# Attention and a two-layer feed-forward block on one core: GpSimd's steps of a head moved to 5 and 7, and the first weights' conversion spread over a pair's 18 steps

## The chip, the core and the metric

The kernel runs on one core of a Trainium2 chip. The metric is the device time of one execution in microseconds (us). The engines are PE (matrix products), DVE, ACT, POOL (GpSimd) and SP (which here only issues DMAs). Each engine works through its own queue in order and waits on semaphores for the others.

## The reference, cut to what matters

All tensors are float64 at the interface; the kernel reads them as pairs of 32-bit words and computes float32-like products from pieces.

```python
# q, k, v: (4, 8, 1152, 64): 32 heads of 1152 keys, 576 pooled queries, 64 channels
q_pool = q.reshape(B, H, S // 2, 2, D).mean(axis=3)
scores = scale * q_pool @ k.T          # 576 x 1152 per head
scores = scores - scores.max(-1)       # softmax over the keys
attn = exp(scores); attn = attn / (attn.sum(-1) + 1e-09)
x = (attn @ v)                         # laid out as 2304 tokens x 512
h = x @ w_in                           # 512 -> 2048
g = s * relu(h) ** 2 + b
out = g @ w_out                        # 2048 -> 512
```

## The kernel before

Heads are worked in 16 pairs. A head is nine steps of 128 keys (`j` = 0 to 8), a pair 18 steps, the attention 288 steps (`n`) and three more to drain. Below, "step 12" means `n % 18 == 12`. The order of every instruction is written out by hand: the main loop over `n` emits them, and `later(k, fn)` with `tick()` puts a piece of work a few steps behind.

In a step PE makes the scores of 128 keys against 576 queries (`score_step`, L486, tile `s`, two buffers of two PSUM banks), one or two products for the row maxima of the pair after this one (`max_unit`, L456, tile `m`, reduced by DVE at L457 into `pm`), and the value products of the step three before (`value_step`, tile `o`, `LAG` = 3). `KIND` says how a step's exponentials are split into a high and a low part:

- "v": ACT makes `ph` (L495) and the full exponential in place in `s` (L498), DVE subtracts to `pl` (L501). Six value products: L524, L526, L528 for each half of the queries.
- "g": ACT makes `ph` and the full exponential `pe` in SBUF, POOL subtracts to `pl`. The same six products.
- "w" (a whole step): ACT makes only `pe` (L490), and PE multiplies it unsplit (L518).

L528 is the product that reads `pl`. At a head's last value product `finish` (steps 2 and 11) has ACT copy the outputs out of PSUM in four pieces (`xu`, `l`, L544 and L545). DVE and POOL then make the inverse and the scaled output (`lt`, `rc`, `rr`, and POOL's `xo` at L564, once per pair).

The pair two ahead is prepared at the steps in `PREP`: DVE transposes (`ka`, `kb`, `qt`), POOL copies and subtracts (`qs` L412, `kh`, `kl` L419, `qh`, `qz`, `ql` L420). `ql` subtracts in place in `qT`. `qm` is a small ACT copy out of `qT` (L212) that the maxima of that pair's first rows need. POOL also splits the values of the next head at steps 7 and 16 (`vv`, `vl`, `prep_v`). SP issues the loads: `kraw` and `qraw` at step 14, `vf` at steps 3 and 12.

In the last six pairs (10 to 15) the loop also converts the first three blocks of float64 weights, one chunk of 128 x 512 numbers per pair. `weights_a()` fetches a chunk one pair ahead (L134, tile `wst`) and runs `narrow` on the one at hand. Its pieces `s0` to `s5` come at the steps in `STA`, counted from the call (0 and 1 both fall in the call's own step, k in the step k - 1 behind). `CB` and `CP` set the calls: step 4 of each of these pairs. So `s0` (ACT: `whm`, `wR`) is at step 4, `s1`, `s1b`, `s1c` (DVE: L159, L163, L166) at step 7, `s2` (DVE L169, ACT L170) at step 9, and POOL's three pieces `s3` (L174), `s4` (L177), `s5` (L180) at steps 12, 14 and 16. Each scratch tile has one buffer.

After the attention the feed-forward block follows (`Moe`), with its own conversion (`weights_b`, `STB`).

Of the kernel before, what the change touches and what calls it, by code (L numbers as in the profile page):

```python
# [12 lines left out]
AF = mybir.ActivationFunctionType  # L13
# [18 lines left out]
KB = 384  # L32


KIND = "vwvgvwvgw" * 2

PP = (("ka", 0), ("kb", 0), ("ha", 0), ("hb", 1), ("qs", 1), ("qt", 1), ("qm", 2), ("qh", 2), ("qz", 2), ("kl", 2), ("ql", 3), ("l0", 7))
PREP = (("qs", 9), ("ka", 10), ("kb", 11), ("ha", 11), ("qt", 12), ("hb", 12), ("kl", 12), ("qm", 13), ("qh", 13), ("qz", 13), ("ql", 14), ("l0", 4), ("l1", 13))
LR = 14
LD = 1  # L40
VS = (7, 16)
XT = (1, 2, 3, 4, 8)
SW = (3, 9)
CB, CP = 274, 18
WB = (7, 11)
STA = (0, 4, 4, 4, 6, 9, 11, 13)
STB = (0, 1, 2, 3, 4, 5, 6, 8)
MO = (2, 3, 6)
XS = (1, 2)
# [3 lines left out]
def f32(ap):  # L53
    return ap.bitcast(F32)
# [3 lines left out]
def attention_moe_kernel(ctx: ExitStack, tc: tile.TileContext, q, k, v, w_in, w_out, s_in, b_in, out):  # L58
    nc = tc.nc
# [35 lines left out]
    def weight_tiles(pool, f0, f1):  # L95
        n = f1 - f0
        ih = pool.tile([P, NC, n * P], F32R, name=f"wih{f0}")
        il = pool.tile([P, NC, n * P], F32R, name=f"wil{f0}")
        oh = pool.tile([P, n, DM], F32R, name=f"woh{f0}")
        ol = pool.tile([P, n, DM], F32R, name=f"wol{f0}")  # L100
        for i in range(n):
            f = f0 + i
            wi_hi[f] = ih[:, :, i * P:(i + 1) * P]
            wi_lo[f] = il[:, :, i * P:(i + 1) * P]
            wo_hi[f] = oh[:, i, :]
            wo_lo[f] = ol[:, i, :]

    def conversions(pool, stage, f0, f1, bufs, stages, psum=None):

        weight_tiles(pool, f0, f1)
        chunks = []
        for f in range(f0, f1):
            chunks.append((w_in[:, f * P:(f + 1) * P].rearrange("(c p) f -> p c f", p=P), wi_hi[f], wi_lo[f], f"i{f}"))
            chunks.append((w_out[f * P:(f + 1) * P, :].rearrange("p (c f) -> p c f", c=NC),
                           wo_hi[f].rearrange("p (c f) -> p c f", c=NC), wo_lo[f].rearrange("p (c f) -> p c f", c=NC), f"o{f}"))
        wide = w_in.dtype == mybir.dt.int64
        raw = {}  # L120
        state = [-1]

        def done(i):
            f = f0 + i // 2
            ready[f] = ready.get(f, 0) + 1

        def tmp(tag, name):
            return stage.tile([P, NC, P], F32, tag=tag, bufs=bufs, name=f"{tag}{name}")

        def fetch(i):  # L130
            src, _, _, name = chunks[i]
            if wide:
                raw[i] = stage.tile([P, NC, 2 * P], I32, tag="wst", bufs=2, name=f"wst{name}")
                nc.sync.dma_start(raw[i], src.bitcast(I32))  # L134
            else:
                raw[i] = stage.tile([P, NC, P], F32, tag="wst", bufs=2, name=f"wst{name}")
                nc.sync.dma_start(raw[i], src)

        def narrow(i):
            _, hi, lo, name = chunks[i]  # L140
            words = raw.pop(i).rearrange("p c (n w) -> p c n w", w=2)
            high, low = words[:, :, :, 1].bitcast(F32), words[:, :, :, 0].bitcast(U32)
            hm, ab, A, R = (tmp(t, name) for t in ("whm", "wab", "wA", "wR")) if psum is None else (None, *(tmp(t, name) for t in ("wab", "wA", "wR")))

            bank = None if psum is None else psum.tile([P, 512], F32, tag="w", bufs=1, name=f"w{name}").rearrange("p (c f) -> p c f", c=NC)
            hm, bits, full = (hm, ab, A) if psum is None else (bank, bank, bank)
            hmi, biti, abi, fulli, top = (t.bitcast(I32) for t in (hm, bits, ab, full, high))
            eng = nc.gpsimd if psum is None else nc.vector

            def s0():  # L150
                nc.scalar.activation(hm, high, AF.Abs)
                if psum is None:
                    nc.scalar.activation(R, low, AF.Copy, scale=2.0 ** -52)
                else:
                    nc.gpsimd.tensor_scalar(out=R, in0=low, scalar1=2.0 ** -52, scalar2=0.0, op0=ALU.mult, op1=ALU.add)

            def s1():

                nc.vector.tensor_scalar(out=hm, in0=hm, scalar1=W_MIN, scalar2=W_MAX, op0=ALU.max, op1=ALU.min)  # L159

            def s1b():

                nc.vector.tensor_scalar(out=biti, in0=hmi, scalar1=0x07FFFFFF, scalar2=3, op0=ALU.bitwise_and, op1=ALU.logical_shift_left)  # L163

            def s1c():
                nc.vector.scalar_tensor_tensor(out=fulli, in0=top, scalar=-0x40000000, in1=biti, op0=ALU.bitwise_and, op1=ALU.bitwise_or)  # L166

            def s2():
                nc.vector.tensor_scalar(out=abi, in0=fulli, scalar1=-0x800000, scalar2=None, op0=ALU.bitwise_and)  # L169
                nc.scalar.activation(hi, full, AF.Copy)  # L170

            def s3():

                nc.gpsimd.tensor_tensor(out=R, in0=R, in1=ab, op=ALU.mult)  # L174

            def s4():
                eng.tensor_tensor(out=A, in0=full, in1=f32(hi), op=ALU.subtract)  # L177

            def s5():
                nc.gpsimd.tensor_tensor(out=lo, in0=A, in1=R, op=ALU.add)  # L180
                done(i)

            for at, fn in zip(stages, (s0, s1, s1b, s1c, s2, s3, s4, s5)):
                later(at, fn)

        def split(i):
            _, hi, lo, _ = chunks[i]
            st = raw.pop(i)
            nc.scalar.activation(hi, st, AF.Copy)

            def rest():
                nc.gpsimd.tensor_tensor(out=lo, in0=st, in1=f32(hi), op=ALU.subtract)
                done(i)

            later(stages[4], rest)

        def go():
            i = state[0]
            if i >= len(chunks):
                return False  # L200
            if i + 1 < len(chunks):
                fetch(i + 1)
            if i >= 0:
                (narrow if wide else split)(i)
            state[0] += 1
            return True

        return go
# [12 lines left out]
    def later(k, fn):  # L221
        step[1] += 1
        queue.append((step[0] + k, step[1], fn))
# [106 lines left out]
    qm = ap.tile([P, P], F32R, name="qm")  # L330
# [149 lines left out]
    def score_step(hd, j, kind):  # L480
        assert holds["k", hd % 3] == holds["c", hd % 3] == hd
        kk, qq = kks[hd % 3], qqs[hd % 3]
        ps = ps_s.tile([P, 2, 512], F32, tag="s", name=f"s{hd}_{j}")
        for a in range(2):
            for i in range(2):
                nc.tensor.matmul(ps[:, a, :HALF], kk[:, i, j * P:(j + 1) * P], qq[:, i, a], start=(i == 0), stop=(i == 1))  # L486
        if kind != "v":
            pe = late.tile([P, 2, HALF], F32, tag="pe", bufs=PE, name=f"pe{hd}_{j}")
        if kind == "w":
            nc.scalar.activation(pe, ps[:, :, :HALF], AF.Exp, scale=SCALE)  # L490
            prob[hd, j] = pe, None
            return
        ph = late.tile([P, 2, HALF], F32R, tag="ph", bufs=PB, name=f"ph{hd}_{j}")
        pl = late.tile([P, 2, HALF], F32R, tag="pl", bufs=PB, name=f"pl{hd}_{j}")
        nc.scalar.activation(ph, ps[:, :, :HALF], AF.Exp, scale=SCALE)  # L495

        full = ps[:, :, :HALF] if kind == "v" else pe
        nc.scalar.activation(full, ps[:, :, :HALF], AF.Exp, scale=SCALE)  # L498
        prob[hd, j] = ph, pl
        eng = nc.vector if kind == "v" else nc.gpsimd  # L500
        fresh.append(lambda: eng.tensor_tensor(out=pl, in0=full, in1=f32(ph), op=ALU.subtract))  # L501
# [115 lines left out]
    lays = {}  # L617
    weights_a = conversions(wa, wstage, 0, SW[0], 1, STA)
    NS = NH * NJ

    for n in range(NS + LAG):
# [5 lines left out]
        for part in ORD[at] if at is not None else "sff":  # L627
            if part == "s" and n < NS:
                score_step(hd, j, KIND[n % 18])
            elif part == "f":  # L630
# [10 lines left out]
        if n < NS:  # L641
# [4 lines left out]
            if n == LD:  # L646
                load_k(2)
                load_q(2)
            if n % 18 == PREP[0][1]:
                lays = {k: prep[k] for k in ("l0", "l1") if k in prep}  # L650
                prep = prep_pair(p + 2) if p + 2 < NPAIR else {}
            for name, at in PREP:

                ops = prep if name not in ("l0", "l1") or at < PREP[0][1] else lays
                if n % 18 == at and name in ops and n >= 8:
# [96 lines left out]
```

## Time and profile before

| | us |
|---|---|
| three runs, median (lowest to highest) | 973.78 (971.0 to 974.75) |
| the profiled execution's own time | 976.95 |
| its span, first to last instruction | 975.2 |
| PE busy in the span | 922.3 (95%) |
| DVE, ACT, POOL busy | 627.0, 545.9, 507.5 |
| PE busy in 20 to 350 us (330 us, pairs without conversion) | 317.55 |
| PE busy in 350 to 525 us (175 us, with conversion) | 158.68 |

The attention runs from about 20 to 557 us, the feed-forward block from there to the end. Where PE is busy nearly all of the time, an idle engine elsewhere costs nothing; what counts is each place where PE stands still, and what it stands still for. A row such as "PE o L528 <- POOL pl L501" says that PE's product at line 528 waited for POOL's subtraction at line 501.

### The profile page before, as it was taken

To read this page: it belongs to the slowest core of one execution; us is meant where nothing else is said; L and a number is where in the kernel's file an instruction comes from. 1 tells how busy PE (TensorE), PEld (TensorE's weight loads), DVE (VectorE), ACT (ScalarE), POOL (GpSimd) and SP (SyncE) were. 2 spreads that over 40 slices of the span, in tenths; PEclk is the share of its full clock that TensorE was granted. 3 is DMA by queue.
4 is the path that set the end of the run, shared out by engine and by line. 5 is a ranking of instruction groups with operands and counts; after the bars stand their busy time and mean duration, and the time that the engine had idled before them with its cause. 6 is when DMAs were issued, how large, how long until landed. Compare 5 with 4: busy or idle time off the path is not lost.

```text
span 975.2 us, 16173 instructions
## 1 busy us (share of the span) xinstructions
PE 922.3 (95%) x5712; PEld 821.4 (84%) x5712; DVE 627.0 (64%) x1168; ACT 545.9 (56%) x1054; POOL 507.5 (52%) x405
## 2 busy tenths in 40 slices
PE   4999999999999998988989989999999999999998
PEld 3888888888888887877877877889999899999997
DVE  5777776777677776876875376776776653334333
ACT  2766666666676675665767755554444443333332
POOL 6567656665667568568665567665353430110000
PEclk9999999999999999999999999999999999999999
DMA  8878776777767776676754155663544332222211
GB/s 149 167 145 169 158 152 122 154 168 147 134 138 167 156 152 147 153 142 138 165 146 102 35 162 164 205 217 130 174 130 158 104 136 78 66 87 90 84 44 44
DMA packets 255312, 131.17 MB, mean 135 GB/s; under 512 B 203776, under 2 KB 227328, under 8 KB 255232
## 3 DMA queue, kind: packets, MB, share of 16 engines
q1 hardware_dynamic: 244512, 129.62, 55.0%
q10 hardware_dynamic: 10720, 0.52, 0.7%
q8 instruction: 46, 0.75, 0.3%
q14 instruction: 34, 0.28, 0.1%
HBM read 68.68 MB, written 18.87 MB: 90 GB/s over the span
## 4 chain that ended last, share of the span: by engine, by line
PE 67%; ACT 12%; POOL 7%; DVE 5%; DMA 3%; issue 3%; ACTq 1%; SPq 0%; DVEq 0%; POOLq 0%
PE h L272 18%; PE y L299 17%; PE s L486 12%; PE o L518 5%; PE m L456 5%; PE o L524 4%; PE o L528 4%; PE o L526 4%; ACT ph L495 3%; ACT xu L544 2%; ACT l L545 2%; ACT s L498 2%; POOL pl L501 1%; DVE pm L457 1%; DMA wsto<-in_moe_w_out_dram 1%
## 5 line engine op out<-in xcount | busy, mean ns | idle before, releaser
L457 DVE TENSOR_REDUCE pm<-m 128x1 f32<-128x384 f32 x432 | 230.6, 549 | 112.8 <-PE m L456 106.9
L486 PE MATMUL s<-qq,kk 128*128 128x288 f32 x1152 | 217.6, 311 | 10.9 <-ACT pe L498 7.8
L272 PE MATMUL h<-x,wih 128*128 128x256 f32 x1152 | 213.3, 283 | 7.1 <-DVE gl L286 6.0
L272 PEld LDWEIGHTS h<-x,wih 128*128 128x128 f32 x1152 | 186.0, 189 | 22.1 <-DVE gl L286 6.4
L495 ACT ACTIVATE ph<-s 128x576 fp32r<-128x576 f32 x192 | 125.2, 652 | 132.4 <-PE s L486 109.8
L486 PEld LDWEIGHTS s<-qq,kk 128*128 128x128 f32 x1152 | 175.6, 191 | 27.2 <-ACT pe L498 11.0
L501 POOL TENSOR_TENSOR pl<-pe,ph 128x576 fp32r<-128x576 f32 x64 | 91.5, 1429 | 141.8 <-ACT pe L498 131.2
L272 PE MATMUL h<-x,wil 128*128 128x256 f32 x576 | 162.2, 282 | 0.0
L456 PE MATMUL m<-kh,qz 128*128 128x384 f32 x384 | 156.9, 418 | 3.2 <-DVE pm L457 3.1
L253 POOL TENSOR_TENSOR x<-xr,x 128x1024 fp32r<-128x1024 f32 x27 | 65.0, 2406 | 152.0 <-ACT x L212 143.1
L280 DVE SCALAR_TENSOR_TENSOR h<-h,sb,r 128x256 f32<-128x256 f32 x144 | 70.2, 487 | 114.5 <-ACT r L289 114.5
L524 PE MATMUL o<-ph,vv 128*128 128x288 f32 x384 | 119.0, 310 | 7.8 <-issue 4.8
L518 PE MATMUL o<-pe,vf 128*128 128x288 f32 x384 | 126.0, 412 | 0.0
L528 PE MATMUL o<-pl,vv 128*128 128x288 f32 x384 | 113.6, 296 | 7.3 <-POOL pl L501 7.3
L289 ACT ACTIVATE r<-h 128x256 f32<-128x256 f32 x144 | 55.6, 386 | 110.0 <-PE h L272 109.8
L501 DVE TENSOR_TENSOR pl<-s,ph 128x576 fp32r<-128x576 f32 x128 | 96.2, 752 | 30.9 <-ACT s L498 24.7
L526 PE MATMUL o<-ph,vl 128*64 128x288 f32 x384 | 113.6, 296 | 0.0
L299 PE MATMUL y<-wol,gh 128*128 128x512 f32 x288 | 113.1, 393 | 0.0
L299 PE MATMUL y<-woh,gl 128*128 128x512 f32 x288 | 112.9, 392 | 0.0
L299 PE MATMUL y<-woh,gh 128*128 128x512 f32 x288 | 112.6, 391 | 0.0
L272 PEld LDWEIGHTS h<-x,wil 128*128 128x128 f32 x576 | 109.6, 190 | 0.0
L283 ACT ACTIVATE gh<-h,sb 128x256 fp32r<-128x256 f32 x144 | 68.0, 473 | 64.6 <-DVE h L280 64.3
(89 smaller groups left out, 1508.6 us busy)
## 6 DMA issues: line engine op xcount, KB each, us to landing
kk<-kh SPq DMA_DIRECT2D x32, 576.0 KB, 6.0
kraw<-in_k_dram SPq DMA_DIRECT2D x64, 144.0 KB, 3.5
vf<-in_v_dram SPq DMA_DIRECT2D x32, 288.0 KB, 4.0
kk<-kT SPq DMA_DIRECT2D x32, 288.0 KB, 4.6
qq<-qh SPq DMA_DIRECT2D x64, 144.0 KB, 5.8
xr<-xd SPq DMA_DIRECT2D x18, 512.0 KB, 4.1
qraw<-in_q_dram SPq DMA_DIRECT2D x122, 72.0 KB, 2.5
wsti<-in_moe_w_in_dram SPq DMA_DIRECT2D x16, 512.0 KB, 4.9
```

The costliest lines, as they stand in the source:

```text
L272: nc.tensor.matmul(h[:, :TB], st[:, c, :], mv[:, c, :], start=(n == 0), stop=(n == 3 * NC - 1))
L280: nc.vector.scalar_tensor_tensor(out=t, in0=h[:, :TB], scalar=sb[:, 0:1], in1=r, op0=ALU.mult, op1=ALU.mult)
L299: nc.tensor.matmul(y[:, :DM], st[:, ts_], mv, start=(first and n == 0), stop=(last and n == 2))
L456: nc.tensor.matmul(ps[:, :KB], st, khs[p][:, e * KB:(e + 1) * KB], start=True, stop=True)
L457: nc.vector.tensor_reduce(out=pms[p][:, col, e:e + 1], in_=ps[:, :KB], axis=AX.X, op=ALU.max)
L486: nc.tensor.matmul(ps[:, a, :HALF], kk[:, i, j * P:(j + 1) * P], qq[:, i, a], start=(i == 0), stop=(i == 1))
L495: nc.scalar.activation(ph, ps[:, :, :HALF], AF.Exp, scale=SCALE)
L501: fresh.append(lambda: eng.tensor_tensor(out=pl, in0=full, in1=f32(ph), op=ALU.subtract))
L518: nc.tensor.matmul(o[:, :HALF], vfs[hd % 2][:, j], ph[:, a], start=first, stop=last)
L524: nc.tensor.matmul(o[:, :HALF], vv[:, j], ph[:, a], start=first, stop=False)
L526: nc.tensor.matmul(o[0:D, :HALF], vl[:, j], ph[:, a], start=False, stop=False)
L528: nc.tensor.matmul(o[:, :HALF], vv[:, j], pl[:, a], start=False, stop=last)
```

## The change

Four edits to the tables and one to `narrow`:

- `KIND`: in each head the steps 3 and 5 change places: 3 is now "w" and 5 "g". The counts stay: four "v", three "w", two "g" per head.
- `PREP`: `qm` goes from step 13 to step 16. It now stands behind `ql` (step 14), so ACT's copy waits for POOL's subtraction and reads what `ql` left in `qT`.
- `CB`: the calls of `weights_a()` go from step 4 to step 0, the fetch with them.
- `STA`: `s0` and `s1` fall in step 0, `s1b` in 2, `s1c` in 4, `s2` in 6; `s3`, `s4`, `s5` in step 17 and in steps 0 and 1 of the next pair.
- `narrow`: ACT's `wR` moves from `s0` to `s2` where the chunk belongs to the attention.

```diff
-KIND = "vwvgvwvgw" * 2
+KIND = "vwvwvgvgw" * 2
-PREP = (..., ("kl", 12), ("qm", 13), ("qh", 13), ("qz", 13), ("ql", 14), ("l0", 4), ("l1", 13))
+PREP = (..., ("kl", 12), ("qm", 16), ("qh", 13), ("qz", 13), ("ql", 14), ("l0", 4), ("l1", 13))
-CB, CP = 274, 18
+CB, CP = 270, 18
-STA = (0, 4, 4, 4, 6, 9, 11, 13)
+STA = (0, 1, 3, 5, 7, 18, 19, 20)
             def s0():
                 nc.scalar.activation(hm, high, AF.Abs)
-                if psum is None:
-                    nc.scalar.activation(R, low, AF.Copy, scale=2.0 ** -52)
-                else:
+                if psum is not None:
                     nc.gpsimd.tensor_scalar(out=R, in0=low, scalar1=2.0 ** -52, scalar2=0.0, op0=ALU.mult, op1=ALU.add)
...
                 nc.scalar.activation(hi, full, AF.Copy)
+                if psum is None:
+                    nc.scalar.activation(R, low, AF.Copy, scale=2.0 ** -52)
```

POOL's queue in a pair with conversion (pair 12, heads 24 and 25; the first number in a name is the head, the second the step of the head; `wRi1`, `wAi1`, `wil0` are the weights' pieces `s3`, `s4`, `s5`), from step 12 on, before:

```order
L501 TENSOR_TENSOR pl25_3_5517<-pe25_3_5515,ph25_3_5516 128x576
L214 TENSOR_SCALAR kh14_5461<-kT14_5458 128x576
L419 TENSOR_TENSOR kT14_5458<-kT14_5458,kh14_5461 128x1152
L174 TENSOR_TENSOR wRi1_5354<-wRi1_5354,wabi1_5352 128x512
L214 TENSOR_SCALAR qh14_5462<-qT14_5459 128x576
L214 TENSOR_SCALAR qz0_101<-qT14_5459 64x512 x2
L420 TENSOR_TENSOR qT14_5459<-qT14_5459,qh14_5462 128x576
L177 TENSOR_TENSOR wAi1_5353<-wAi1_5353,wih0_265 128x512
L501 TENSOR_TENSOR pl25_7_5630<-pe25_7_5628,ph25_7_5629 128x576
L214 TENSOR_SCALAR vv0_105<-vf0_103 128x9x64
L180 TENSOR_TENSOR wil0_266<-wAi1_5353,wRi1_5354 128x4x128
```

and now:

```order
L214 TENSOR_SCALAR kh14_5463<-kT14_5460 128x576 x2
L419 TENSOR_TENSOR kT14_5460<-kT14_5460,kh14_5463 128x1152
L214 TENSOR_SCALAR qh14_5464<-qT14_5461 128x576
L214 TENSOR_SCALAR qz0_101<-qT14_5461 64x512 x2
L501 TENSOR_TENSOR pl25_5_5569<-pe25_5_5567,ph25_5_5568 128x576
L420 TENSOR_TENSOR qT14_5461<-qT14_5461,qh14_5464 128x576
L501 TENSOR_TENSOR pl25_7_5622<-pe25_7_5620,ph25_7_5621 128x576
L214 TENSOR_SCALAR vv0_105<-vf0_103 128x9x64
L431 TENSOR_TENSOR vl0_107<-vf0_103,vv0_105 128x576
L174 TENSOR_TENSOR wRi1_5259<-wRi1_5259,wabi1_5257 128x512
L177 TENSOR_TENSOR wAi1_5258<-wAi1_5258,wih0_265 128x512
L180 TENSOR_TENSOR wil0_266<-wAi1_5258,wRi1_5259 128x4x128
```

The step "g" of the second head that stood first now stands behind the six preparation instructions, `s3` and `s4` have left the stretch, and `vl` is no longer behind `s5`.

ACT's queue behind the four copies of `finish`, at step 12 of pair 11 (head 23; L471 and L472 are the DMAs that send the maxima of a coming head), before:

```order
L495 ACTIVATE ph23_3_5089<-s23_3_5083 128x576
L498 ACTIVATE pe23_3_5088<-s23_3_5083 128x576
L471 DMA qq0_97<-c24_5102 1x128x4
L472 DMA qq0_97<-c24_5102 1x64x1
L495 ACTIVATE ph23_4_5122<-s23_4_5117 128x576
L498 ACTIVATE s23_4_5117<-s23_4_5117 128x2x288
L212 ACTIVATE qm_100<-qT13_5032 64x64 x2
L490 ACTIVATE pe23_5_5147<-s23_5_5142 128x576
```

and now:

```order
L490 ACTIVATE pe23_3_5088<-s23_3_5083 128x576
L471 DMA qq0_97<-c24_5099 1x128x4
L472 DMA qq0_97<-c24_5099 1x64x1
L495 ACTIVATE ph23_4_5117<-s23_4_5112 128x576
L498 ACTIVATE s23_4_5112<-s23_4_5112 128x2x288
L495 ACTIVATE ph23_5_5141<-s23_5_5135 128x576
L498 ACTIVATE pe23_5_5140<-s23_5_5135 128x576
L495 ACTIVATE ph23_6_5178<-s23_6_5173 128x576
L498 ACTIVATE s23_6_5173<-s23_6_5173 128x2x288
L495 ACTIVATE ph23_7_5194<-s23_7_5188 128x576
L498 ACTIVATE pe23_7_5193<-s23_7_5188 128x576
L212 ACTIVATE qm_100<-qT13_5034 64x64 x2
```

One exponential instead of two stands between the copies and the next step, and `qm` (L212) stands behind the two of step 16.

DVE's queue in pair 12 from step 4 on (`rr` is the transposition of the inverse, `pm` the maxima), before:

```order
L501 TENSOR_TENSOR pl24_4_5332<-s24_4_5326,ph24_4_5331 128x576
L560 STREAM_TRANSPOSE rr11_5357<-rc11_5324 128x576
L457 TENSOR_REDUCE pm13_5310<-m13_3_5367 128x1
L457 TENSOR_REDUCE pm13_5310<-m13_4_5387 128x1
L457 TENSOR_REDUCE pm13_5310<-m13_5_5393 128x1
L501 TENSOR_TENSOR pl24_6_5383<-s24_6_5377,ph24_6_5382 128x576
L457 TENSOR_REDUCE pm13_5310<-m13_6_5410 128x1
L159 TENSOR_SCALAR whmi1_5351<-whmi1_5351 128x512
L163 TENSOR_SCALAR wabi1_5352<-whmi1_5351 128x512
L166 SCALAR_TENSOR_TENSOR wAi1_5353<-wsti1_4922,wabi1_5352 128x512
```

and now (line numbers are two lower):

```order
L501 TENSOR_TENSOR pl24_4_5337<-s24_4_5331,ph24_4_5336 128x576
L164 SCALAR_TENSOR_TENSOR wAi1_5258<-wsti1_4827,wabi1_5257 128x512
L560 STREAM_TRANSPOSE rr11_5355<-rc11_5329 128x576
L457 TENSOR_REDUCE pm13_5316<-m13_3_5368 128x1
L457 TENSOR_REDUCE pm13_5316<-m13_4_5389 128x1
L457 TENSOR_REDUCE pm13_5316<-m13_5_5393 128x1
L501 TENSOR_TENSOR pl24_6_5385<-s24_6_5379,ph24_6_5384 128x576
L167 TENSOR_SCALAR wabi1_5257<-wAi1_5258 128x512
```

The three pieces that stood together behind step 6's `pl` are apart: `wAi1` (`s1c`) is now between step 4's `pl` and `rr`, `wabi1` (`s2`) behind step 6's `pl`; `whmi1` and the first `wabi1` stand earlier, at steps 0 and 2.

## Rows read from the trace of the kernel before

**Rows 1.** The waits of PE, whole span: total us, times, longest.

```profile
PE s L486 <- ACT pe L498: 7.8, 14, 0.6
PE o L528 <- POOL pl L501: 7.3, 4, 2.1
...
PE m L456 <- DVE pm L457: 3.1, 5, 0.7
```

**Rows 2.** Timeline of POOL, line L564: start us, duration us, instruction, idle before.

```profile
69.69 1.43 POOL L564 TENSOR_TENSOR xo<-xu,rr 128x576 f32<-128x576 f32 x1 [1.48 <-DVE rr L560]
...
358.85 1.43 POOL L564 TENSOR_TENSOR xo<-xu,rr 128x576 f32<-128x576 f32 x1 [1.49 <-DVE rr L560]
...
502.91 1.43 POOL L564 TENSOR_TENSOR xo<-xu,rr 128x576 f32<-128x576 f32 x1 [1.20 <-DVE rr L560]
```

**Rows 3.** Timeline of POOL, pair 12, 444 to 456 us.

```profile
444.13 1.42 POOL L501 TENSOR_TENSOR pl<-pe,ph 128x576 fp32r<-128x576 f32 x1 [1.71 <-ACT pe L498]
...
448.89 1.30 POOL L174 TENSOR_TENSOR wRi<-wRi,wabi 128x512 f32<-128x512 f32 x1
...
454.56 1.28 POOL L177 TENSOR_TENSOR wAi<-wAi,wih 128x512 f32<-128x512 f32 x1
```

**Rows 4.** Busy time of two stretches: us, each engine, PEclk, DMA share, GB/s.

```profile
386.00:390.00 4.00, 4.00 (x16) 3.41 (x15) 0.87 (x2) 2.75 (x7) 2.69 (x3) 0.57 0.16 26
457.00:461.00 4.00, 3.75 (x14) 3.16 (x15) 0.56 (x1) 2.65 (x5) 3.43 (x4) 0.63 0.37 58
```

**Rows 5.** Timeline of all engines, pair 6, 240 to 254 us.

```profile
240.37 0.77 DVE L413 STREAM_TRANSPOSE kT<-kraw 128x576 f32<-128x576 f32 x1
...
243.92 0.67 POOL L214 TENSOR_SCALAR kh<-kT 128x576 fp32r<-128x576 f32 x1
...
246.08 0.65 ACT L490 ACTIVATE pe<-s 128x576 f32<-128x576 f32 x1
...
247.94 2.29 POOL L214 TENSOR_SCALAR qz<-qT 64x512 fp32r<-64x512 f32 x2
...
249.70 0.69 PE L486 MATMUL s<-qq,kk 128*128 128x288 f32 x4
...
250.31 1.41 POOL L420 TENSOR_TENSOR qT<-qT,qh 128x576 f32<-128x576 f32 x1
...
253.04 0.69 PE L486 MATMUL s<-qq,kk 128*128 128x288 f32 x4
...
254.01 0.29 PE L528 MATMUL o<-pl,vv 128*128 128x288 f32 x1
```

**Rows 6.** Timeline of all engines, pair 7, 274 to 279 us.

```profile
274.40 0.65 ACT L498 ACTIVATE pe<-s 128x576 f32<-128x576 f32 x1
...
275.10 0.80 PE L486 MATMUL s<-qq,kk 128*128 128x288 f32 x4 [0.56 <-ACT pe L498]
...
275.44 0.73 ACTq L472 DMA_DIRECT2D qq<-c  x1
...
276.22 0.65 ACT L495 ACTIVATE ph<-s 128x576 fp32r<-128x576 f32 x1 [1.18 <-PE s L486]
...
277.44 0.76 DVE L501 TENSOR_TENSOR pl<-s,ph 128x576 fp32r<-128x576 f32 x1 [0.30 <-ACT s L498]
...
278.55 0.69 PE L486 MATMUL s<-qq,kk 128*128 128x288 f32 x4
```

**Rows 7.** Timeline of DVE and POOL in pairs 10 and 12.

```profile
363.76 0.69 DVE L166 SCALAR_TENSOR_TENSOR wAi<-wsti,wabi 128x512 int32<-128x512 int32 x1
...
434.45 1.73 DVE L166 SCALAR_TENSOR_TENSOR wAi<-wsti,wabi 128x512 int32<-128x512 int32 x1
...
438.16 0.68 POOL L214 TENSOR_SCALAR vv<-vf 128x576 fp32r<-128x576 f32 x1 [2.53 <-DMA vf<-in_v_dram]
```

**Rows 8.** DMA issues of the page: tile, KB each, us to landing.

```profile
vf<-in_v_dram SPq DMA_DIRECT2D x32, 288.0 KB, 4.0
...
wsti<-in_moe_w_in_dram SPq DMA_DIRECT2D x16, 512.0 KB, 4.9
```

More of the change, by code (lines that the diff above doesn't have):

```diff
@@ L32 @@
 KB = 384
-KIND = "vwvgvwvgw" * 2
+KIND = "vwvwvgvgw" * 2
 PP = (("ka", 0), ("kb", 0), ("ha", 0), ("hb", 1), ("qs", 1), ("qt", 1), ("qm", 2), ("qh", 2), ("qz", 2), ("kl", 2), ("ql", 3), ("l0", 7))
-PREP = (("qs", 9), ("ka", 10), ("kb", 11), ("ha", 11), ("qt", 12), ("hb", 12), ("kl", 12), ("qm", 13), ("qh", 13), ("qz", 13), ("ql", 14), ("l0", 4), ("l1", 13))
+PREP = (("qs", 9), ("ka", 10), ("kb", 11), ("ha", 11), ("qt", 12), ("hb", 12), ("kl", 12), ("qm", 16), ("qh", 13), ("qz", 13), ("ql", 14), ("l0", 4), ("l1", 13))
 LR = 14
```

## The prediction

> **What bounds the kernel now.** Read first PE's waits over the whole span [rows 1]. PE is the engine that sets the time, and only three waits of it have to do with what is edited: scores (L486) that wait for the second exponential of a "g" step, 7.8 us in 14 places; the product L528 that waits for POOL's `pl`, 7.3 us in only 4 places of up to 2.1 us; and maxima (L456) that wait for DVE, 3.1 us in 5 places.
>
> The second view is POOL's timeline of `xo`, which comes once per pair at step 5 and so is a clock of the pairs [rows 2]. From pair 1 to pair 10 it advances 358.85 - 69.69 = 289.16 us in nine pairs, 32.13 us each. The next four pairs, 10 to 13, take 502.91 - 358.85 = 144.06 us, 36.02 each. These four hold both a conversion and the preparation of a coming pair. Their excess is 144.06 - 4 x 32.13 = 15.5 us, twice what the waits of POOL alone show.
>
> The third view, POOL's queue in one of them, tells why [rows 3]. Step 12's `pl` starts at 444.13, and step 16's can start only when `s4` ends, at 455.84. In between stand `s3` (1.30 us) and `s4` (1.28 us), 2.58 us that an ordinary pair has not, and PE stands still for about 2 us. Two of the four stops also lower its granted clock: it averages 0.57 and 0.63 of full speed over 4 us, mostly the lower of its two levels, 1.2 GHz [rows 4]. 0.43 x 4 + 0.37 x 4 us make 3.2 us. So the excess per pair is about 1.8 us of waiting for `pl`, 0.6 for DVE's maxima, 0.8 for the clock in the mean, and some 0.7 of pieces restarting late.
>
> **The change part by part.** *The conversion's POOL pieces.* `s3`, `s4`, `s5` leave steps 12 to 16 for 17, 0 and 1. Behind step 16's `vl` POOL now has nothing until step 5, five steps of 32.13 / 18 = 1.78 us, so their 3.9 us (three times about 1.3 us) fit before step 5's `pl`. What is late next in these pairs is not step 16's `pl`, but step 14's.
>
> *Step 14's `pl`.* This is the edit that could hurt, in all 14 pairs with preparation: the step "g" moves behind `kh`, `kl`, `qh`, `qz`. In an ordinary pair [rows 5] the second `kh` starts at 243.92 and `qz` ends at 250.23, a run of 6.31 us without a gap. What held it to 243.92 was step 12's `pl`, which is gone; its input, DVE's transposition, ends at 240.37 + 0.77 = 241.14. The run then goes from 241.2 to 247.5. The exponential of step 14 ends at about 246.08 + 0.65 = 246.73 (the slot that is now "g" has one more exponential there, but `qm` has left the slot before it), so `pl` runs from 247.5 to 248.9. PE wants it at step 17: its scores start at 249.70, and the product that reads `pl` comes 254.01 - 253.04 = 0.97 us behind the scores of such a step, at 250.67. Slack 1.7 us: nothing lost. If the cover went (a run that starts at 243.92 as now) `pl` would end at 251.6 and PE lose 0.9 us a pair.
>
> *`qm` at step 16.* ACT now waits there for `ql`. `ql` (1.41 us, rows 5) follows `pl`, so ends at 250.3. Step 16's exponentials end two steps behind step 14's, also at 246.73 + 3.57 = 250.3, so ACT hardly waits. Queued behind the copy is step 17's exponential, which then ends near 251.5 (half a microsecond for the copy, 0.65 for itself). It is wanted by the scores at 253.04: hidden.
>
> *The "w" behind the head's end.* Steps 2 and 11 load ACT with `finish`; the next step has now one exponential less. At 275.10 [rows 6] the scores had waited 0.56 us for the exponential that started at 274.40; the only one now starts 0.55 earlier (where the first of the two did), so this wait goes. But ACT's next exponential cannot follow: it stands behind L472, whose issue ends at 276.17 and which follows DVE's maxima, not ACT. DVE's `pl` still ends at 278.20, and the scores two steps on, at 278.55, need it. So they move to about 278.33, and 0.22 of the 0.56 us is kept: 14 x 0.22 = 3.1 us. Bounds: 0, where L472 is longer, and 7.8, if the whole wait goes.
>
> *DVE's pieces apart.* In step 4 `s1c` now stands between `pl` and `rr`, a block of 0.76 [rows 6] + 0.69 [rows 7] + 0.77 (a transposition, rows 5) = 2.2 us ahead of a maximum; before, three pieces in a row at step 7, one of them of 1.73 us, cost PE about 0.6 us (3.1 in 5 places). I keep that 0.6 us as not saved, and add 0.3 for `s2` beside POOL's work of steps 5 and 7; bounds of both together 0 and 1.6 us.
>
> On one of these pieces, DVE's `s1c` (L166), the rows show 0.69 us alone and 1.73 us beside POOL's `pl` [rows 7]. The Trainium skill ("SBUF — State Buffer", section "SBUF: two separate sides") says that DVE and GpSimd share a port pair as an exclusive lock, so that a DVE operation with two SBUF inputs blocks until GpSimd's is through. The trace agrees; by that rule `s1c` at step 4, where POOL is now idle, costs 0.69, and it is `s1` and `s2`, beside POOL at steps 0 and 6, that may be held up to 1.3 us each. If PE felt all of one of these, four pairs would give back 5 us, and the sum below would end at 965.
>
> *The fetch, four steps earlier.* SP's queue is held by `qraw` into step 4, so the 512 KB fetch now goes out right ahead of `vf`, and POOL's `vv` at step 7 waits for `vf`. Before, `vv` waited up to 2.53 us in these pairs [rows 7] with no fetch ahead. The cost is between 0 and the fetch's whole landing, 4.9 us [rows 8]; the 224 KB that it is larger than a `vf` cost 0.9 us, from which I estimate 2.1 us for 512 KB. Behind `vv` stand `vl`, `qs`, both `kh`, `kl`, `qh`, `qz`, then step 14's `pl`. In pair 12, where `vv` had waited 2.53 us, POOL was still 1.71 us idle ahead of step 12's `pl` [rows 3], and step 14's has 1.7 us of slack, so 2 us more should cost PE between nothing and 1.3 us. I take 0.5 us a pair.
>
> *Sum.* Of the 15.5 us of the four pairs I leave 4 x (0.6 + 0.3 + 0.5) = 5.6 us standing: 9.9 saved. With 3.1 at the heads' ends, 13.0 us. The profiled execution took 976.95 us (span 975.2 and 1.75 around it), so it would take 964; it lies 3.2 us above the median of the runs shown, 973.78. The saving set against that median gives 960.8, and I say 961. From the bounds, the four pairs keep 0 to 4 x (1.6 + 1.3) = 11.6 us and so save 15.5 to 3.9, the heads' ends 7.8 to 0: 950.5 to 969.9.
>
> **The rivals.** (1) *The fetch ahead of `vf` becomes the new stop.* The fetch delays `vf` by its whole landing, step 14's `pl` is 1.6 us late in each of the four pairs, and the clock falls again (0.8 each). For it: the wait of 2.53 us that is there already. Against: a `vf` lands in 4.0 us in the median, and DMAs share the way. Of 15.5 us 4 x (0.9 + 1.6 + 0.8) = 13 stay; with 3 at the heads' ends: 968.
>
> (2) *The whole head-end wait goes and the four pairs become ordinary ones.* For it: 14 equal waits of 0.56 us that all end with one exponential. Against: L472 stands behind it and does not move. 15.5 + 7.8 less 1: 952.
>
> (3) *POOL's work only changes places.* The wait for `pl` moves from step 19 to step 17 in the four pairs, at the same price; the change does not do what it says. For it: POOL's sum of work per pair is unchanged. Against: the five steps behind step 16 stand empty for it. With a saving of 1 to 2 us at the heads' ends: 972.
>
> (4) *Slower: step 14's `pl` is late in every pair.* It decides from a run of six that starts later than 241.2 + 1.7 = 242.9. At a start 1.5 us behind that PE loses 1.5 us in 14 pairs, 21 us; against 13 us saved this is 8 us more: 982. For it: POOL goes in order and has nothing between the first `kh` and the second, so any late input of these six instructions is handed on. Against: the inputs are the same as now and end at 241.14.
>
> **How the numbers follow.** About 0.5% is what a measurement of this kernel tells from no change; here 4.9 us. Chances: forecast 0.55 (its own range 955 to 966), (1) 0.15, (2) 0.13, (3) 0.10, (4) 0.07. Faster by over 0.5% (below 968.9): the forecast, (2), and most of (1): 0.82. The same: (3) and the rest of (1), 0.11. Slower 0.07. The range that leaves out 2 in 10: 951 to 970.
>
> **What would show it right or wrong.** Right: `xo` in pairs 10 to 13 advances by 33 to 34 us in place of 36; no wait of L528 for POOL above 0.6 us; PEclk at 1.00 all through; the scores' 0.56 us waits gone or turned into short ones for DVE's `pl`; `xo` in the pairs before at 31.6 to 32.0. Wrong: PE waiting for POOL at step 17 (rivals 1 and 4), `vv` waiting for `vf` by over 4 us (1), or the same period as before in the ordinary pairs with a wait on DVE of 0.5 us in each (the head-end term).

## The result: 964.6 us, and the profile after

The changed kernel took 964.60 us in the median of 4 runs (960.31 to 966.07), against 974.26 of the kernel before on the same chip: a ratio of 0.9896, interval 0.9875 to 0.9918. Run a second time beside another set of kernels it took 963.59 us (0.9893, interval 0.9877 to 0.9909). The forecast was 961, the range 951 to 970. The profiled execution took 960.31 us (span 958.4), the fastest of its four runs, and that of before was slower than every timed run of its kernel; so 16.6 us lie between the two profiles, where the medians bear out 10. So sizes below are taken from the pairs inside the traces, where the two profiles of the changed kernel repeat within 0.1 us in the nine ordinary pairs together and 1.5 us in the four conversion pairs together, and from medians.

PE's waits over the whole span, of the kernel after, answer to [rows 1] (total, times, longest):

```profile
PE s L486 <- DVE pl L501: 7.9, 18, 1.9
PE m L456 <- DVE pm L457: 0.8, 1, 0.8
PE s L486 <- ACT pe L498: 0.6, 1, 0.6
```

The wait of L528 for POOL (7.3 us in [rows 1]) is gone from the list, and that for the maxima has one place left. The 7.8 us of waiting for one exponential are gone too, but 7.9 us of waiting for DVE's `pl` stand in the list; 6.6 of them, in 13 places, are of the scores of step 15, two steps behind those that had waited before. POOL's `xo`, which counts the pairs as in [rows 2], says where this matters (start, duration, operation):

```profile
69.43 1.43 POOL L564 TENSOR_TENSOR xo<-xu,rr 128x576 f32<-128x576 f32 x1
...
360.97 1.44 POOL L564 TENSOR_TENSOR xo<-xu,rr 128x576 f32<-128x576 f32 x1
...
490.37 1.43 POOL L564 TENSOR_TENSOR xo<-xu,rr 128x576 f32<-128x576 f32 x1
```

From pair 10 to pair 14 it is now 129.40 us, 32.35 a pair, where it was 144.06 and 36.02: 14.7 us less (13.1 in the second profile, where they took 130.93). From pair 1 to pair 10 it is 291.54 us, where it was 289.16: 2.4 us *more*. The conversion pairs became ordinary ones, and the ordinary ones became slower.

POOL's queue in conversion pair 12 shows the first half, beside [rows 3] and [rows 7]:

```profile
431.78 0.67 POOL L214 TENSOR_SCALAR vv<-vf 128x576 fp32r<-128x576 f32 x1 [2.11 <-DMA vf<-in_v_dram]
...
439.95 2.28 POOL L214 TENSOR_SCALAR qz<-qT 64x512 fp32r<-64x512 f32 x2
442.32 1.43 POOL L501 TENSOR_TENSOR pl<-pe,ph 128x576 fp32r<-128x576 f32 x1
443.70 1.43 POOL L420 TENSOR_TENSOR qT<-qT,qh 128x576 f32<-128x576 f32 x1
445.09 1.43 POOL L501 TENSOR_TENSOR pl<-pe,ph 128x576 fp32r<-128x576 f32 x1
446.48 0.69 POOL L214 TENSOR_SCALAR vv<-vf 128x576 fp32r<-128x576 f32 x1
447.25 1.42 POOL L431 TENSOR_TENSOR vl<-vf,vv 128x576 fp32r<-128x576 f32 x1
448.64 1.46 POOL L174 TENSOR_TENSOR wRi<-wRi,wabi 128x512 f32<-128x512 f32 x1
450.06 1.29 POOL L177 TENSOR_TENSOR wAi<-wAi,wih 128x512 f32<-128x512 f32 x1
451.42 1.29 POOL L180 TENSOR_TENSOR wil<-wAi,wRi 128x512 fp32r<-128x512 f32 x1
```

The three conversion pieces stand in one row behind `vl`, no `pl` waits for them, and `vv` still waits 2.11 us for `vf` with the larger fetch ahead of it, without PE waiting for POOL behind it. (In the second profile of this kernel PE waits there once, for 0.56 us; see the account of the fetch below.) The granted clock is 1.00 over the whole stretch of these pairs (before: 0.57 and 0.63 at two of the stops, [rows 4]); columns are each engine's busy time, then PEclk, DMA share and GB/s:

```profile
350.00:525.00 175.00, 167.91 (x1041) 148.07 (x1039) 138.29 (x248) 126.31 (x233) 120.79 (x97) 1.00 0.72 152
```

The second half is seen at the head's end of an ordinary pair, where [rows 6] showed a wait of 0.56 us. Of the kernel after, ACT with its queue, then DVE, then PE, in pair 6:

```profile
241.04 0.65 ACT L490 ACTIVATE pe<-s 128x576 f32<-128x576 f32 x1
242.12 0.49 ACTq L471 DMA_DIRECT2D qq<-c  x1
242.70 0.85 ACTq L472 DMA_DIRECT2D qq<-c  x1
243.61 0.65 ACT L495 ACTIVATE ph<-s 128x576 fp32r<-128x576 f32 x1 [1.92 <-PE m L456]
244.15 0.65 ACT L498 ACTIVATE s<-s 128x576 f32<-128x576 f32 x1
...
244.83 0.76 DVE L501 TENSOR_TENSOR pl<-s,ph 128x576 fp32r<-128x576 f32 x1 [1.03 <-ACT s L498]
...
245.74 0.76 PE L486 MATMUL s<-qq,kk 128*128 128x288 f32 x4 [0.37 <-DVE pl L501]
```

The scores two steps further on wait for `pl`, and `pl` waits for two exponentials that could start only when L472 was issued, at 243.55. To see what such a wait costs, the starts of all scores (L486) were read from the timelines: a pair has 18 intervals, and interval i is the one in which PE takes the products of step i (it begins with the scores of step i+3). Medians of eight ordinary pairs, in us:

| intervals | before | after |
|---|---|---|
| 2, 3, 4, 5 | 1.49, 1.77, 1.50, 1.85 | 1.57, 1.92, 1.57, 1.75 |
| 9, 10, 11 (head's end) | 3.32, 1.56, 1.89; together 6.77 | 2.78, 1.57, 2.43; together 6.78 |
| 12 to 17, together | 9.88 | 9.93 |

All 0.54 us that interval 9 won are back in interval 11, and intervals 2 to 5 lost 0.2 us. The expectations below count steps in this way where they give a step's time (the step of an operation, as `ql` at 16, is the program's own).

### The profile page after: what moved, and what is told of

Same layout as the page of the kernel before. It is cut to its first block, busy times and chain, and to the rows that moved or that the text cites. A ratio compares the mean times of both kernels' runs of the same rounds, so it can differ in the third digit from the quotient of the medians.

```text
span 958.4 us, 16192 instructions
## 1 busy us (share of the span) xinstructions
PE 917.9 (96%) x5712; PEld 816.5 (85%) x5712; DVE 626.2 (65%) x1168; ACT 544.9 (57%) x1054; POOL 506.0 (53%) x405
## 4 chain that ended last, share of the span: by engine, by line
PE 70%; DVE 9%; ACT 8%; DMA 4%; issue 2%; ACTq 2%; SPq 2%; POOL 2%; DVEq 0%; POOLq 0%
PE h L272 18%; PE y L299 18%; PE s L486 12%; PE o L518 6%; PE m L456 5%; PE o L524 4%; PE o L526 4%; PE o L528 4%; DVE pl L501 3%; DVE pm L457 3%; ACT ph L495 2%; ACT s L498 2%; ACT xu L544 1%; ACTq L472 1%; ACT l L545 1%
## 5 line engine op out<-in xcount | busy, mean ns | idle before, releaser
L486 PE MATMUL s<-qq,kk 128*128 128x288 f32 x1152 | 217.0, 310 | 9.3 <-DVE pl L501 7.9
L486 PEld LDWEIGHTS s<-qq,kk 128*128 128x128 f32 x1152 | 172.5, 189 | 29.1 <-PE o L528 8.7
L456 PE MATMUL m<-kh,qz 128*128 128x384 f32 x384 | 154.3, 411 | 0.8 <-DVE pm L457 0.8
L518 PE MATMUL o<-pe,vf 128*128 128x288 f32 x384 | 123.2, 405 | 0.0
L528 PE MATMUL o<-pl,vv 128*128 128x288 f32 x384 | 112.7, 294 | 0.0
```

The lines of the kernel that those rows point to most:

```text
L456: nc.tensor.matmul(ps[:, :KB], st, khs[p][:, e * KB:(e + 1) * KB], start=True, stop=True)
L518: nc.tensor.matmul(o[:, :HALF], vfs[hd % 2][:, j], ph[:, a], start=first, stop=last)
L528: nc.tensor.matmul(o[:, :HALF], vv[:, j], pl[:, a], start=False, stop=last)
```

## The experiments

Each edit is against the kernel named. "Ordinary" is `xo` from pair 1 to 10, "conversion" from pair 10 to 14; before they were 289.16 and 144.06 us.

**The conversion alone** (the kernel after, with two numbers put back):

```
-KIND = "vwvwvgvgw" * 2
+KIND = "vwvgvwvgw" * 2
-... ("qm", 16) ...
+... ("qm", 13) ...
```

> The kernel before with the conversion taken apart (STA, CB, the place of the R copy), and with the old KIND and qm at 13. Theory A (from the two traces: the four conversion pairs lost 14.4 us in all, and the new KIND costs every ordinary pair 0.2 to 0.3 us): xo advances 32.0 to 32.1 us in the ordinary pairs, 32.2 to 33.0 in pairs 10 to 13, no L528 wait for POOL above 0.6 us, and the time is 2 to 4 us below the changed kernel's 964.6: 961 to 962.5. Theory B (as predicted: the conversion gives 9.9, the head ends 3.1): 3 us above the changed kernel, about 967.5. Theory C (the conversion's gain needs KIND, since step 12's pl and POOL's row behind it stay): pairs 10 to 13 at 34 to 35 us and 970.

960.91 us (959.48 to 962.50), ratio 0.9861, interval 0.9832 to 0.9889. Its `xo`:

```profile
68.65 1.43 POOL L564 TENSOR_TENSOR xo<-xu,rr 128x576 f32<-128x576 f32 x1 [1.49 <-DVE rr L560]
...
358.04 1.42 POOL L564 TENSOR_TENSOR xo<-xu,rr 128x576 f32<-128x576 f32 x1 [2.10 <-DVE rr L560]
...
488.81 1.42 POOL L564 TENSOR_TENSOR xo<-xu,rr 128x576 f32<-128x576 f32 x1 [1.74 <-PE o L524]
```

Ordinary 289.39 as before, conversion 130.77. The conversion's part alone gives 13.3 us, more than the whole change. Theory A held; B, the sizes as predicted, fell.

**KIND and `qm` alone** (the same two numbers changed in the kernel before):

> The kernel before with KIND and qm at 16 alone. Theory A: xo advances 32.3 us in the ordinary pairs in place of 32.03 to 32.13, the 0.56 us waits of the scores for ACT go and come back two steps later as waits for DVE's pl, pairs 10 to 13 keep at least 34.5 us, and the time is 2 to 4 us above before (974.3): 976 to 978. Theory B (0.22 us kept at each head's end): ordinary pairs at 31.9, 971. Theory C (the new places of g give POOL room too): pairs 10 to 13 fall to 34 us, 968.

974.11 us, ratio 0.9994 (0.9979 to 1.001): no change, which none of the three had. The trace shows two effects of opposite sign. Ordinary pairs took 290.99 us (+1.8); conversion pairs 139.97 (-4.1). PE's waits in it:

```profile
PE s L486 <- DVE pl L501: 6.6, 13, 1.8
PE m L456 <- DVE pm L457: 6.2, 6, 1.3
...
PE o L528 <- POOL pl L501: 1.4, 8, 0.2
```

With `g` at step 14 POOL's `pl` is hardly waited for even with the conversion's pieces in its way, and half of what that saves is lost at DVE. Beside the spread conversion little of those 4 us is left to win: the conversion pairs took 129.40 and 130.93 us in two profiles with the new KIND, 130.77 and 130.41 in two without. KIND's cost in the ordinary pairs remains.

**`qm` back at 13** (the kernel after, `("qm", 16)` to `("qm", 13)`):

> The changed kernel with qm back at step 13. Theory A (ACT's wait of qm for ql at step 16, 13.9 us in 14 places, stands beside other work; the 0.07 us delays of three steps per pair come from DVE's pl behind two maxima, not from qm): ordinary pairs stay at 32.3, time within 1 us of the changed kernel. Rival D (the wait holds step 17's exponential and with it three steps): ordinary pairs 32.0 to 32.1, 3 us faster. Rival E (at 13 the copy stands ahead of step 14's exponential, behind which POOL's pl follows): PE waits for POOL's pl, 0.3 to 0.9 us in each of 14 pairs, 4 to 12 us slower.

962.31 us (0.9873, 0.9845 to 0.9901), ordinary 292.14, conversion 129.69: theory A, no cost and no gain within the measurement. ACT's wait for `ql` was hidden. One more thing speaks for 13: `ql` subtracts in place, so at 16 the copy takes what `ql` leaves in `qT`, and the shift of a head's last 64 queries is taken from the remainder and no longer from the values. As the time is the same, the earlier place is the better one.

**Only POOL's pieces moved** (the kernel before):

```
-STA = (0, 4, 4, 4, 6, 9, 11, 13)
+STA = (0, 4, 4, 4, 6, 14, 15, 16)
```

> The kernel before with only POOL's s3, s4, s5 of the conversion moved behind step 16 (steps 18, 19, 20 of the pair's count, that is 0, 1, 2 of the next); DVE's three pieces stay in one row at step 8, fetch, KIND and qm stay. Theory A (POOL's stops and the lost clock made 2.6 of the 3.6 us excess a pair, DVE's row about 0.6 to 0.9): pairs 10 to 13 at 32.8 to 33.3 us, 974.3 - 11 = 963. Rival F (DVE's row, beside POOL's work, holds PE for more once POOL no longer stops it): pairs at 34 to 35 us, 968 to 971.

By the rule of `STA`, the pieces fall in step 17 and in steps 0 and 1, as in the kernel after, and DVE's row in step 7; the expectation counts one more. 964.31 us (0.9898, 0.9874 to 0.9923): conversion 133.78, ordinary 288.84. POOL's pieces are 10.3 of the 13.3 us. The other 3.0, 0.75 us a pair, belong to what the first experiment changes besides: DVE's row taken apart, and with it the earlier fetch and the place of `wR`, which no run tells apart. It is a balance: interval 6, where PE waits behind the row, falls from 2.44 to 1.50 us, and interval 3 rises from 1.75 to 2.26. Of PE's waits the maxima remain:

```profile
PE m L456 <- DVE pm L457: 3.4, 5, 0.7
```

**The row of maxima sent from SP's queue** (the kernel after; L471 and L472 alike):

```
-nc.scalar.dma_start(f32(row[D:D + 1, :NT4 * P]), f32(c[:, full]))
+nc.sync.dma_start(f32(row[D:D + 1, :NT4 * P]), f32(c[:, full]))
```

> The changed kernel with the two sends of the maxima's row (L471, L472) issued from SP's queue in place of ACT's. Theory A (the head end is held by the chain c, L472's issue on ACT, ph, DVE's pl; the 0.56 us wait for one exponential is not the limit): ph no longer stands behind L472, the scores' step 11 goes from 2.4 to 1.9 us, step 9 stays at 2.78, ordinary pairs go from 32.30 to about 31.75, and the time from 964.6 to 957. Rival G (the limit is DVE's row of maxima ahead of pl, whatever ACT does): step 11 stays at 2.3 to 2.4, 964. Rival H (SP's queue, busy with qraw and the layouts, sends the row late): a new wait of the scores at a head's first step, 970 or more.

965.32 us (0.9916, 0.9900 to 0.9931): no faster, yet the head's end did what theory A said. In a pair whose interval 9 begins at 248.16 (SP's queue, ACT, DVE, PE):

```profile
251.87 0.59 SPq L472 DMA_DIRECT2D qq<-c  x1
...
251.49 0.65 ACT L495 ACTIVATE ph<-s 128x576 fp32r<-128x576 f32 x1 [0.60 <-PE s L486]
...
252.71 0.76 DVE L501 TENSOR_TENSOR pl<-s,ph 128x576 fp32r<-128x576 f32 x1
...
254.10 0.69 PE L486 MATMUL s<-qq,kk 128*128 128x288 f32 x4
```

The `ph` starts 3.33 us behind the interval's start in place of 4.64, `pl` ends at 5.31 in place of 6.62, and the scores start at 5.94 in place of 6.77, without a wait: 0.83 us a pair. But the ordinary pairs fell only to 32.11 us, since intervals 15 to 17 gave 0.7 us back (ACT's `qm` now waits 1.75 to 1.79 us for `ql` there in every pair, 24.6 us in 14 places where the kernel after had 13.9, which is the likely cause), and at the start of the program SP's queue made a new stop of 9.0 us. So the new wait of H came too, though not its 970 us.

**The same on the conversion alone:**

> The kernel with the conversion alone changed (961), with the two sends issued from SP's queue. Theory A: with the old KIND the 0.56 us wait for the second exponential of step 9 stays (step 9 at 3.32), step 11 is at 1.89 already: ordinary pairs stay at 32.03; pairs 10 to 13, where step 11 was 2.7, keep the same sum or lose up to 0.5 us; 959 to 961. Rival G2 (ACT is freed by a microsecond for each head and all its exponentials come earlier): ordinary pairs 31.5, 954. Rival H as for the changed kernel: 968 or more.

964.08 us (0.9903, 0.9887 to 0.9919), ordinary pairs 31.90 to 31.93 us. PE's waits, and SP's queue in the first pairs:

```profile
PE s L486 <- issue: 8.8, 1, 8.8
PE o L528 <- POOL pl L501: 6.1, 14, 0.5
```

```profile
18.84 4.40 SPq L358 DMA_DIRECT2D qraw<-in_q_dram  x8
...
28.11 0.78 SPq L407 DMA_DIRECT2D qq<-qT  x1
28.98 0.54 SPq L471 DMA_DIRECT2D qq<-c  x1
```

The first head's row stands behind eight loads of `qraw` and the second head's layout (in the kernel before ACT sends it at 20.09); that is the 8.8 us of H, with 964 in place of its 968. Interval 9 fell to 2.60, where A wanted 3.32: a miss. Which of the score banks the scores of step 13 take is fixed when the program is built. In the kernel before it is the one that step 12's exponential on ACT releases; with the sends on SP it is the one that DVE's `pl` of step 11 releases, earlier: in the traces these scores wait for a semaphore that ACT raises in the one, DVE in the other. The wait of 0.56 us was for a bank, not for ACT as such. In the four conversion pairs of the first experiment the same bank is taken, with the sends still on ACT, and intervals 9 to 11 are 2.60, 1.45 and 2.72 us in the mean: 6.77 again. So the wait can go in two ways, and neither shortens the head's end. Where the sends leave ACT, with new KIND and with old, it is 5.94. In the new KIND the scores that had waited for `pl` of step 13 still take its bank, so there the sends alone made the difference.

**The new KIND in the second half alone, and in the first alone:**

```
KIND = "vwvgvwvgw" + "vwvwvgvgw"     (with qm at 16)
KIND = "vwvwvgvgw" + "vwvgvwvgw"     (with qm at 13)
```

> The changed kernel with the new KIND in the second half alone (steps 9 to 17; steps 0 to 8 as before): KIND = vwvgvwvgw + vwvwvgvgw. Theory A (in the first half the new places of w and g make DVE's pl late by 0.07 us in steps 2 to 5, 0.18 us a pair; in the second half the 0.54 us of step 9 come back as 0.53 in step 11, and 0.08 more): ordinary pairs 32.10 to 32.15, time 962 (between 961 without either half and 964.6 with both). Rival (all of the 0.27 us is of the second half, whose w is the one that was moved beside the preparation): ordinary pairs 32.3, 964 to 965.

> The kernel with the conversion alone changed, and the new KIND in the first half alone: KIND = vwvwvgvgw + vwvgvwvgw, qm at 13. Theory A: ordinary pairs 32.20 to 32.22 with steps 2, 3, 4, 5 at 1.57, 1.92, 1.57, 1.75, and step 9 back at 3.32; in pairs 10 to 13 the step 3 of 2.27 us (DVE's pl behind the conversion's pieces) falls to 1.92, 32.3 to 32.5 there; time 962 to 963. Rival (the first half is free of cost): ordinary pairs 32.03 and 960.

964.26 us (0.9899, 0.9880 to 0.9918) and 962.55 us (0.9889, 0.9870 to 0.9908). In the first half the cost is as A said: intervals 2 to 5 at 1.57, 1.92, 1.57, 1.75 and pairs of 32.2 to 32.4 us, 290.65 in all, 1.3 us above the run without; three of the four are 0.07 to 0.15 us longer than before and one 0.1 shorter, 0.2 us a pair together; why was not taken further. The new order has its use there too: in the conversion pairs interval 3 takes 1.92 us here and in the kernel after, 2.26 in the first experiment. The second half was a miss in both directions. Five of eight ordinary pairs took 31.90 to 32.08 us, no more than before, but three took 32.64 to 33.36. In those L472's issue was long. ACT's queue and PE in the slowest:

```profile
338.53 1.90 ACTq L472 DMA_DIRECT2D qq<-c  x1
340.47 0.65 ACT L495 ACTIVATE ph<-s 128x576 fp32r<-128x576 f32 x1 [2.89 <-PE m L456]
...
342.61 0.76 PE L486 MATMUL s<-qq,kk 128*128 128x288 f32 x4 [1.36 <-DVE pl L501]
```

With 0.72 us (interval 11 is then 2.21) the head's end is 0.2 us shorter than before, with 1.90 us it is 1.0 longer. That is the head-end term as it is: it hangs on the issue of one DMA. The traces also show what goes with a long issue. In pairs 1 to 13 of the ten runs that send from ACT, L472 took 0.47 to 0.62 us in all 145 places where no layout of a coming head's keys (L404, `kk`) was still on its way, and over 0.62 us in 108 of 115 places where one was (median 0.85). Whether that copy is the cause was not tried.

**Both kernels once more on one chip:**

> The changed kernel once more, on the same chip as the kernel with the conversion alone, so that KIND and qm can be told from the chip and the day. Theory A (KIND costs an ordinary pair 0.27 us, 13 pairs 3.5 us, less 0.8 us that the conversion pairs win by it): 2 to 4 us above the next run, about 964. Rival (the difference of 3.7 us between the two medians was the session): within 1 us of the next run.

> The kernel before with the conversion alone changed, once more: 961 by theory A, ordinary pairs 32.03 to 32.06, pairs 10 to 13 at 32.6; by the rival the same as the changed kernel.

963.59 us (960.99 to 964.24) and 961.23 us (960.59 to 962.31; 0.9875, 0.9862 to 0.9889). The difference of 2.4 us has the sign and size of theory A, but the intervals overlap, so the medians alone do not prove it. The traces do repeat: ordinary 291.45 against 289.51 us, with 291.54 and 289.39 the first time.

**The sends from SP's queue except those of the first two heads, and then also `ql` behind step 16's `pl`** (both on the conversion alone; the second adds the last two lines):

```
-nc.scalar.dma_start(
+(nc.scalar if hd < 2 else nc.sync).dma_start(
-... ("ql", 14) ...
+... ("ql", 16) ...
```

> The kernel with the conversion alone changed, and the two sends of the row from SP's queue for all heads but the first two. Theory A (the single stop of 8.8 us at the start came from SP's queue, where the second head's row stood behind the loads of k and q; the head end itself is 0.83 us shorter without ACT's issue, and 0.7 of it is given back at step 16, where PE waits for POOL's pl): the 8.8 us stop is gone, ordinary pairs 31.90, pairs 10 to 13 at 32.4, the time 2 us below the kernel with the conversion alone: 959. Rival: the stop stays or moves to the third head, 963 or more.

> As the run before, with POOL's ql at step 16, behind that step's pl, in place of 14. Theory A (at step 16 pl ends 1.41 us late-to-need because ql stands ahead of it in POOL's queue): pl ends 1.41 us earlier, step 16 falls from 2.2 to 1.5 us, ordinary pairs 31.2 us, pairs 10 to 13 at 31.7, the time 8 to 9 us below the run before: 950. Rival 1 (vv and vl, now 1.41 us later, hold the product of the next head's first step): a new wait there and 955 to 960. Rival 2 (DVE's or ACT's work is late next at step 12 or 16): ordinary pairs 31.5 to 31.9, 955 to 959.

955.28 us (0.9813, 0.9799 to 0.9826) and **948.37 us** (0.9748, 0.9731 to 0.9765), against 973.41 of the kernel before on the same chip. The second beats both kernels, by 25 us and by 15. In the first the stop at the start is gone, and this is what bounds the ordinary pairs (31.9 us), PE's wait and POOL's row in one of them:

```profile
PE o L528 <- POOL pl L501: 5.7, 13, 0.4
```

```profile
245.62 2.32 POOL L214 TENSOR_SCALAR qz<-qT 64x512 fp32r<-64x512 f32 x2
248.02 1.42 POOL L420 TENSOR_TENSOR qT<-qT,qh 128x576 f32<-128x576 f32 x1
249.41 1.42 POOL L501 TENSOR_TENSOR pl<-pe,ph 128x576 fp32r<-128x576 f32 x1
```

In the second `pl` follows `qz` at once:

```profile
242.18 2.30 POOL L214 TENSOR_SCALAR qz<-qT 64x512 fp32r<-64x512 f32 x2
244.56 1.43 POOL L501 TENSOR_TENSOR pl<-pe,ph 128x576 fp32r<-128x576 f32 x1
245.95 1.43 POOL L420 TENSOR_TENSOR qT<-qT,qh 128x576 f32<-128x576 f32 x1
```

L528 waits for POOL no more, interval 16 falls from 2.20 to 1.50 us, and ordinary pairs take 31.21 us, the 31.2 that was expected. Of pairs 10 to 13 the first takes 31.7 us as expected, the others 32.2, with 0.55 us more in interval 1; that is open.

The Trainium skill ("Trainium Kernel Development and Optimization", section "Key Constraints") says that issuing DMAs from several engines "only saves the sequencer's issue time". The runs agree, and show what that can be worth: L471 and L472 hold ACT's row for 0.49 and 0.85 us in the pair shown above, and taking them off it made the difference between 961.23 and 955.28 us. Of the 5.9 us between the two profiles 1.6 lie in the ordinary pairs, 0.8 in the conversion pairs, 1.6 in pairs 14 and 15 and 0.4 ahead of pair 1; the last 1.5 lie behind the last `xo`, in work that the edit does not touch, so about 4.4 us are the edit's.

## Why the prediction held, and where its steps failed

The time fell into the range and close to the forecast, because two terms were wrong in opposite directions; that much of it was luck. The larger term had its mechanism right; the smaller one, booked as a gain, came out as a loss.

*The conversion pairs* (forecast 9.9 us saved): the mechanism was right, the size too small; 13.3 and 12.2 us in the two runs of it alone. POOL's pieces saved 10.3 of it by themselves. The term that was mis-sized is the 5.6 us left standing. The 0.6 us a pair for DVE's maxima does not stay: in the kernel after, no maximum of these pairs waits for DVE. With the old KIND 0.5 us a pair is lost at another place, interval 3, which takes 2.26 us in the first experiment. The 0.3 us for pieces beside POOL's work does not appear. The 0.5 us for the fetch is nearly nothing, but not because the fetch does no harm: `vf` took 6.6 to 7.1 us from issue to landing in these pairs, against 3.6 to 5.1 where only POOL's pieces were moved and the fetch stayed behind it, and 4.4 to 7.1 in the kernel before. On average that is 2.6 and 1.2 us more, and 2.1 had been estimated. `vv` waited 1.3 to 2.55 us, and the slack ahead of PE took it in seven of the eight pairs of the two profiles. In pair 12 of the second profile `vv` waited longer than anywhere in [rows 7], and PE then stood still (in the run with `qm` back at 13, once for 0.67 us in the same pair):

```profile
434.39 0.67 POOL L214 TENSOR_SCALAR vv<-vf 128x576 fp32r<-128x576 f32 x1 [3.66 <-DMA vf<-in_v_dram]
...
446.43 0.40 PE L528 MATMUL o<-pl,vv 128*128 128x288 f32 x1 [0.56 <-POOL pl L501]
```

*Step 14's `pl`* came out on the numbers: it was to run from 247.5 to 248.9 behind a run of six that begins at 241.2. In POOL's timeline of that pair:

```profile
241.06 0.67 POOL L214 TENSOR_SCALAR kh<-kT 128x576 fp32r<-128x576 f32 x1 [1.61 <-DVE kT L413]
...
247.46 1.43 POOL L501 TENSOR_TENSOR pl<-pe,ph 128x576 fp32r<-128x576 f32 x1
```

The product that reads it starts at 250.13, which leaves 1.2 us of slack where 1.7 were forecast. So rivals 1, 3 and 4 fell: no stop took the old one's place in the first profile and one of 0.56 us in the second, POOL's work did find room, and step 14 is in time in the ordinary pairs. Rival 2 was right on the four pairs and wrong on the heads' ends.

*The DVE piece beside POOL*: the forecast allowed that `s1` or `s2` is held up to 1.3 us. It is another piece that is held most, `s1b` at step 2 (L161; POOL, then DVE, in pair 11):

```profile
387.11 1.28 POOL L180 TENSOR_TENSOR wil<-wAi,wRi 128x512 fp32r<-128x512 f32 x1
...
387.57 1.11 DVE L161 TENSOR_SCALAR wabo<-whmo 128x512 int32<-128x512 int32 x1
```

The same piece takes 0.42 us at 354.99, where POOL is idle; here it ends 0.3 us behind POOL's. It took 1.02 to 1.12 us in pairs 11 to 13; there `s1` took 0.76 or 0.77 us and `s2` 0.42. The lock that the Trainium skill tells of ("SBUF — State Buffer", section "SBUF: two separate sides") fits that, if this piece, which reads one SBUF input and not two, runs in one of the two-port modes that the section also names; no run here shows its mode. PE has no wait for DVE between 386 and 400, so PE did not feel it. The 965 us that the prediction gave for that case is close to the 964.6 measured, but by chance: what was lost was lost in the ordinary pairs.

*The heads' ends* (forecast 3.1 us saved): this step failed. The part that it called the next limit, L472, `ph`, `pl`, was the right one, and the runs with the sends on SP show it. But it took its duration from one place, 0.73 us in [rows 6], where the pairs of the kernel before have 0.56 to 1.41, and counted 0.13 us from the end of `pl` to the scores. In the kernel after, `c` comes 0.07 us later behind the interval's start, L472 takes 0.83 to 1.02 us in the nine ordinary pairs, and the scores start 0.15 us behind `pl`: 6.78 us from the interval's start, as before. The 0.22 us was inside the scatter of one DMA's issue. The bound of 0, "where L472 is longer", was the answer, and the sign that had been named for it, the old period with a wait on DVE of half a microsecond in each pair, is nearly what the trace shows: the wait is 0.32 to 0.56 us, and the pairs took 32.39 us, longer than before and not the 31.6 to 32.0 of the forecast. Why the issue is longer is not settled. The cost that KIND brings to intervals 2 to 5 was missed altogether: the forecast looked at the second half of the pattern alone, though the pattern changes in both.

## What to carry to other kernels

A wait at the bottleneck engine names who released it, not what would limit next: before a gain is booked for it, follow the chain behind it and take the scatter of each link from all its places. When a stop is removed in a few places and an order is changed in all, try the two apart; here the best version keeps the one and drops the other. A DMA issue in the row of an engine that computes is work of that engine, and may be moved to a queue that has nothing urgent, if what stands ahead of it there at the program's start is looked at too.

## What the hardware showed beyond this

At the first head's end of pairs 1 to 13 the issue of L472 took 0.56 to 1.90 us on ACT's queue, and on SP's queue 0.59 or 0.60 us in 8 to 11 of these 13 pairs, depending on the run, and up to 1.18 in the others. Which bank the scores take decided which engine they waited for, while the length of the stretch stayed at 6.77 us.
